# T5 attention and a max-of-three FFN on one core: head pairs on one array, bias as exponential factors in a band, replicated softmax sums, converting loads, and FFN chunks between score tiles

## The chip, the core and the metric

The kernel runs on one core of one Trainium2 chip. The core has TensorE (PE; its weight loads are listed as PEld), VectorE (DVE), ScalarE (ACT), GpSimd (POOL) and SyncE (SP); SP, ScalarE and POOL can issue DMAs. The metric is the device time of one execution in microseconds, the median of several runs.

## The reference

Attention with a T5 relative-position bias over 8 batches, 8 heads, 576 positions and a head size of 64, and behind it a feed-forward layer (FFN) whose hidden value is the largest of three products.

```
scores = q @ k.T / sqrt(64)                    # per batch and head, 576 x 576
n      = abs(i - j)
bucket = n                if n < 16
         16 + int(15 * log(n / 16) / log(8)), at most 31, otherwise
scores = scores + bias_table[bucket, head]
attn   = exp(scores - max) / (sum + 1e-9)
x      = (attn @ v), heads side by side        # 4608 tokens x 512
h      = max(x @ w1, x @ w2, x @ w3)           # 4608 x 768
out    = h @ w_out                             # 4608 x 512, float32
```

All inputs are float32. Both kernels compute in bfloat16 with float32 sums, and neither subtracts the maximum.

## The kernel before

Setup (L78 to L154). VectorE writes the bias of every distance, for 8 heads, into one row per head (L120); the row goes to DRAM (L127), and 40 transfers on SP and POOL bring it back as 40 bias tiles, one for each head and each of the five tiles of 128 keys (the last has 64), with keys in reverse order (L139). The four weights are loaded as float32 and converted by VectorE (L149, L154).

A head (`attention_head`, L158) runs in these steps.

- Loads: q on SP (L162, L165), k on ScalarE's queue (L166, L169), v on POOL (L170, L173), as float32; VectorE converts (L177 to L201).
- Transposes on TensorE: q against the identity (L186), k and v against a reversing matrix (L196, L207), each into the one PSUM buffer with the tag `tp`, copied out by VectorE or ScalarE (L191, L197, L208).
- For each of five key tiles: the scores, 128 keys by 576 queries, as matmuls of 512 and 64 columns that use 64 rows of the array (L215); VectorE adds the bias tile into float32 (L221); ScalarE takes the Exp into bfloat16 (L225); TensorE multiplies by v with a column of ones, 65 columns of the array, so that the last row of `ot` holds the sums (L229).
- Normalisation: VectorE copies the row of sums (L238), TensorE turns it into columns (L241), VectorE takes reciprocals and widens them to 64 columns (L247, L251), TensorE turns these back into rows (L257), ScalarE copies the outputs (L261), and VectorE multiplies (L264, L267) into `xT` and, for the last 64 tokens of the batch, into `xtail`.

The FFN of a batch is a list of 10 units: six first-stage units (L272: three products of four matmuls of 512 columns, L279, and the running maximum on VectorE, L287, L290, L293) and four second-stage units (L296: six matmuls, L301, a copy on ScalarE, L308, stores on SP, L310). `hook` (L346) runs one unit of the batch before behind every fourth score tile. Score tiles and FFN products share the two PSUM buffers of the tag `st`. The FFN of the last batch and that of the 512 tail tokens run at the end (L356, L358).

The order within each queue is made by the framework from the order of the program and its own estimate of when operands are ready; it also places the semaphores.

Of the kernel before, what the change touches and what calls it, by code (L numbers as in the profile page):

```python
# [39 lines left out]
def kernel(  # L41
# [17 lines left out]
    assert d_model == H * D and S == 576 and D == 64 and NB == 32  # L59
    NQT = 5  # L60
    WLEN = 2 * S - 1
    inv_sqrt_d = 1.0 / float(np.sqrt(D))
    KTILES = [(0, 128), (128, 128), (256, 128), (384, 128), (512, 64)]
    FCH = d_ff // 128
    DCH = d_model // 128
# [3 lines left out]
    biasp = ctx.enter_context(tc.tile_pool(name="biasp", bufs=1))  # L69
    headio = ctx.enter_context(tc.tile_pool(name="headio", bufs=2))  # L70
    headw = ctx.enter_context(tc.tile_pool(name="headw", bufs=2))
    xtp = ctx.enter_context(tc.tile_pool(name="xtp", bufs=2))
    ffnw = ctx.enter_context(tc.tile_pool(name="ffnw", bufs=2))
    psum = ctx.enter_context(tc.tile_pool(name="psum", bufs=1, space=bass.MemoryType.PSUM))
    psum2 = ctx.enter_context(tc.tile_pool(name="psum2", bufs=2, space=bass.MemoryType.PSUM))
    dram = ctx.enter_context(tc.tile_pool(name="dram", bufs=1, space=bass.MemoryType.DRAM))

    ident = const.tile([P, P], F32, name="ident")  # L78
    make_identity(nc, ident[:])
    ident_bf = const.tile([P, P], BF16, name="ident_bf")  # L80
    nc.vector.tensor_copy(ident_bf[:], ident[:])
    jrev = const.tile([P, P], BF16, name="jrev")
    jrev_f = const.tile([P, P], F32, name="jrev_f")
# [4 lines left out]
    )  # L88
    nc.vector.tensor_copy(jrev[:], jrev_f[:])
    jrev64 = const.tile([64, 64], BF16, name="jrev64")  # L90
    jrev64_f = const.tile([64, 64], F32, name="jrev64_f")
    nc.gpsimd.memset(jrev64_f[:], 0.0)
    nc.gpsimd.affine_select(
        out=jrev64_f[:], in_=jrev64_f[:], compare_op=ALU.not_equal, fill=1.0,
        base=-63, pattern=[[1, 64]], channel_multiplier=1,
    )
    nc.vector.tensor_copy(jrev64[:], jrev64_f[:])

    ones1 = const.tile([1, P], BF16, name="ones1")
    nc.vector.memset(ones1[:], 1.0)  # L100

    tableT = const.tile([H, NB], F32, name="tableT")
    tbl_src = bass.AP(
        tensor=bias_table.tensor, offset=bias_table.offset, ap=[[1, H], [H, NB]],
    )
    nc.sync.dma_start(out=tableT[:], in_=tbl_src)

    w_f = stage.tile([H, WLEN], F32, name="w_f", tag="w_f")
    nc.gpsimd.memset(w_f[:], 0.0)
    ranges = _bucket_ranges(S, NB, 128)  # L110
    for vv, rg in enumerate(ranges):
        if rg is None:
            continue
        lo, hi = rg
        segs = [(S - 1 + lo, S - 1 + hi)]
        lo2 = max(lo, 1)
        if hi > lo2:
            segs.append((S - 1 - hi + 1, S - 1 - lo2 + 1))
        for (m0, m1) in segs:
            nc.vector.tensor_scalar(  # L120
                out=w_f[:, m0:m1], in0=w_f[:, m0:m1], scalar1=tableT[:, vv : vv + 1],
                scalar2=8.0, op0=ALU.add, op1=ALU.mult,
            )
    w_sb = const.tile([H, WLEN], BF16, name="w_sb")
    nc.vector.tensor_copy(w_sb[:], w_f[:])
    w_dr = dram.tile([H, WLEN], BF16, name="w_dr")
    nc.sync.dma_start(out=w_dr[:], in_=w_sb[:])  # L127

    bias_tiles = [[None] * NQT for _ in range(H)]
    ei = 0  # L130
    for h in range(H):
        for t, (jt, kp) in enumerate(KTILES):
            bt = biasp.tile([P, S], BF16, name=f"bias_{h}_{t}", tag=f"bias_{h}_{t}")
            src = bass.AP(
                tensor=w_dr.tensor,
                offset=w_dr.offset + h * WLEN + (S - jt - kp),
                ap=[[1, kp], [1, S]],
            )
            (nc.sync if ei % 2 == 0 else nc.gpsimd).dma_start(out=bt[0:kp, :], in_=src)  # L139
            ei += 1  # L140
            bias_tiles[h][t] = bt

    w_bfs = []
    for wi, wk in enumerate((moe_w1, moe_w2, moe_w3)):
        st_w = stage.tile([P, DCH, d_ff], F32, name=f"wst{wi}", tag=f"wst{wi}")
        eng = nc.sync if wi % 2 == 0 else nc.scalar
        eng.dma_start(out=st_w[:], in_=wk.rearrange("(c p) f -> p c f", p=P))
        wb = const.tile([P, DCH, d_ff], BF16, name=f"w{wi}_bf")
        nc.vector.tensor_copy(wb[:], st_w[:])  # L149
        w_bfs.append(wb)  # L150
    wo_st = stage.tile([P, FCH, d_model], F32, name="wost", tag="wost")
    nc.gpsimd.dma_start(out=wo_st[:], in_=moe_w_out.rearrange("(c p) m -> p c m", p=P))
    wo_bf = const.tile([P, FCH, d_model], BF16, name="wo_bf")
    nc.vector.tensor_copy(wo_bf[:], wo_st[:])  # L154

    out_flat = out

    def attention_head(b, h, xT, xtail, hook):  # L158
        q_st = headio.tile([P, NQT, D], F32, tag="q_st")
# [45 lines left out]
        for t, (jt, kp) in enumerate(KTILES):  # L205
            jm = jrev if kp == 128 else jrev64
            nc.tensor.matmul(vr[0:kp, t, :], lhsT=jm[:, :], rhs=v_bf[0:kp, t, :])  # L207
# [182 lines left out]
```

## Time and profile before

| | |
|---|---|
| median of 3 runs | 1168.22 us (1166.13 to 1168.84) |
| profiled execution, first to last instruction | 1165.3 us |
| TensorE busy | 768.9 us, 66% |
| TensorE weight loads | 371.7 us, 32% |
| VectorE busy | 634.5 us, 54% |
| ScalarE busy | 320.6 us, 28% |
| POOL busy | 106.0 us, 9% |
| mean granted clock of TensorE | 0.740 |
| HBM read and written | 39.91 MB and 9.46 MB |

The page gives for the profiled execution its span alone, which is taken as its own time here. A row of the groups reads: line, engine, operation, output and inputs, shapes, count; then busy time in us and mean ns of one; then the engine's idle time before these instructions and what ended it. A row of the timeline reads: start, duration, engine, line, operation, count, and in brackets the idle time before it. Durations of consecutive matmuls overlap, so their pace is read from their starts. Shapes of matmuls begin with rows*columns of the array that they use.

### The profile page before, as it was taken

To read this page: it belongs to the slowest core of one execution; us is meant where nothing else is said; L and a number is where in the kernel's file an instruction comes from. 1 tells how busy PE (TensorE), PEld (TensorE's weight loads), DVE (VectorE), ACT (ScalarE), POOL (GpSimd) and SP (SyncE) were. 2 spreads that over 40 slices of the span, in tenths; PEclk is the share of its full clock that TensorE was granted. 3 is DMA by queue.
4 is the path that set the end of the run, shared out by engine and by line. 5 is a ranking of instruction groups with operands and counts; after the bars stand their busy time and mean duration, and the time that the engine had idled before them with its cause. 6 is when DMAs were issued, how large, how long until landed. Compare 5 with 4: busy or idle time off the path is not lost.

```text
span 1165.3 us, 11325 instructions
## 1 busy us (share of the span) xinstructions
PE 768.9 (66%) x3684; PEld 371.7 (32%) x3744; DVE 634.5 (54%) x1770; ACT 320.6 (28%) x485; POOL 106.0 (9%) x224
## 2 busy tenths in 40 slices
PE   0356666666667676666767666676766677676697
PEld 0123333333333333333333333333333333333333
DVE  4455555655555545564556545564555645565464
ACT  0233322232322232223322233222322233222311
POOL 2410000000000000000000000000000000000000
PEclk9999996765776667675667657766676756776599
DMA  7821111011101111101110111111111011100002
GB/s 247 195 65 32 30 31 31 16 40 49 35 21 31 35 49 30 29 18 50 49 26 21 31 47 41 26 26 36 52 31 26 21 49 49 26 21 1 18 27 64
DMA packets 94035, 50.12 MB, mean 43 GB/s; under 512 B 81488, under 2 KB 84816, under 8 KB 93976
## 3 DMA queue, kind: packets, MB, share of 16 engines
q1 hardware_dynamic: 48120, 24.71, 7.7%
q10 hardware_dynamic: 39440, 11.02, 4.1%
q0 software_dynamic: 6416, 13.67, 4.0%
q8 instruction: 29, 0.48, 0.2%
q14 instruction: 30, 0.25, 0.1%
HBM read 39.91 MB, written 9.46 MB: 42 GB/s over the span
## 4 chain that ended last, share of the span: by engine, by line
PE 51%; DVE 25%; ACT 9%; DMA 8%; issue 5%; ACTq 1%; SPq 0%; DVEq 0%; POOL 0%
PE ps L279 15%; PE ot L229 10%; DVE s_sb L221 7%; ACT e_bf L225 7%; DMA k_st<-in_k_dram 6%; PE tpq L186 4%; PE rb L257 4%; PE tpk L196 4%; PE st L215 4%; DVE xt L264 4%; DVE denrow L238 4%; DVE qT L191 2%; PE dcol L241 2%; ACT kT L197 2%; PE vr L207 2%
## 5 line engine op out<-in xcount | busy, mean ns | idle before, releaser
L225 ACT ACTIVATE e_bf<-s_sb 128x576 bf16<-128x576 f32 (+1 forms) x320 | 216.2, 682 | 367.3 <-DVE s_sb L221 220.0
L221 DVE TENSOR_TENSOR s_sb<-st,bias 128x576 f32<-128x576 f32 (+1 forms) x320 | 234.4, 753 | 94.1 <-PE st L215 81.1
L229 PE MATMUL ot<-e_bf,vb 128*65 128x512 bf16 (+3 forms) x640 | 173.3, 365 | 78.0 <-ACT e_bf L225 72.5
L215 PE MATMUL st<-qT,kT 64*128 64x512 bf16 (+3 forms) x640 | 171.9, 379 | 33.0 <-DVE s_sb L221 20.6
L279 PE MATMUL ps<-xt,w_bf 128*128 128x512 bf16 x540 | 176.7, 454 | 10.4 <-issue 5.9
L229 PEld LDWEIGHTS <-vb 128*65 128x65 bf16 (+1 forms) x640 | 80.4, 135 | 193.3 <-issue 184.5
L197 ACT ACTIVATE kT<-tpk 64x576 bf16<-64x576 f32 x64 | 41.2, 644 | 276.4 <-PE tpk L196 276.4
L186 PE MATMUL tpq<-ident_bf,q_bf 128*64 128x128 bf16 (+1 forms) x320 | 52.4, 302 | 94.1 <-DVE xtail L267 61.6
L170 POOL DMA_DIRECT2D v_st<-in_v_dram x64 | 50.6, 791 | 641.2 <-DVE v_bf L201 582.9
L279 PEld LDWEIGHTS <-w_bf 128*128 128x128 bf16 x648 | 63.8, 112 | 93.7 <-issue 54.3
L215 PEld LDWEIGHTS <-kT 64*128 64x128 bf16 (+1 forms) x640 | 53.7, 113 | 123.2 <-issue 115.7
L238 DVE CAST denrow<-ot 1x576 bf16<-1x576 f32 x64 | 48.1, 752 | 74.0 <-PE ot L229 73.8
L196 PE MATMUL tpk<-jrev,k_bf 128*64 128x128 bf16 (+1 forms) x320 | 49.3, 290 | 39.4 <-DVE qT L191 39.4
L287 DVE COPY cur<-ps 128x512 f32<-128x512 f32 x54 | 37.4, 692 | 69.3 <-PE ps L279 59.5
L257 PE MATMUL rb<-ident_bf,rrep 128*64 128x128 bf16 (+1 forms) x320 | 50.1, 278 | 35.4 <-DVE rrep L251 35.4
L186 PEld LDWEIGHTS <-q_bf 128*64 128x64 bf16 (+1 forms) x320 | 33.0, 151 | 113.0 <-DVE xtail L267 69.7
L207 PE MATMUL vr<-v_bf,jrev 128*128 128x64 bf16 (+1 forms) x320 | 35.9, 238 | 48.4 <-ACT kT L197 48.4
L264 DVE TENSOR_TENSOR xt<-o_sb,rb 64x512 bf16<-64x512 f32 x64 | 43.5, 680 | 35.0 <-PE rb L257 35.0
L261 ACT ACTIVATE o_sb<-ot 64x576 f32<-64x576 f32 x64 | 41.1, 643 | 76.8 <-DVE denrow L238 76.8
L208 DVE CAST vb<-vr 128x256 bf16<-128x256 f32 x64 | 27.3, 426 | 64.0 <-PE vr L207 64.0
L191 DVE COPY qT<-tpq 64x576 bf16<-64x576 bf16 x64 | 28.8, 450 | 56.5 <-PE tpq L186 56.5
L241 PE MATMUL dcol<-ones,denrow 1*128 1x1 bf16 (+1 forms) x320 | 24.1, 169 | 45.5 <-DVE denrow L238 45.5
(115 smaller groups left out, 580.8 us busy)
## 6 DMA issues: line engine op xcount, KB each, us to landing
k_st<-in_k_dram ACTq DMA_DIRECT2D x64, 128.0 KB, 2.2
v_st<-in_v_dram POOLq DMA_DIRECT2D x64, 128.0 KB, 2.7
q_st<-in_q_dram SPq DMA_DIRECT2D x64, 128.0 KB, 2.2
out_dram<-osb SPq DMA_DIRECT2D x32, 256.0 KB, 2.0
wst<-in_moe_w_dram SPq DMA_DIRECT2D x2, 1536.0 KB, 16.7
bias<-w_dr SPq DMA_DIRECT2D x16, 144.0 KB, 6.9
bias<-w_dr POOLq DMA_DIRECT2D x16, 144.0 KB, 8.0
wst<-in_moe_w_dram ACTq DMA_DIRECT2D x1, 1536.0 KB, 10.0
```

Source lines behind the costliest of these rows:

```text
L186: nc.tensor.transpose(tpq[:, 128 * t : 128 * t + rows], q_bf[0:rows, t, :], ident_bf[0:rows, 0:rows],)
L196: nc.tensor.matmul(tpk[:, jt : jt + kp], lhsT=k_bf[0:kp, t, :], rhs=jm[:, :])
L197: nc.scalar.activation(out=kT[:], in_=tpk[:], func=ACTF.Copy)
L207: nc.tensor.matmul(vr[0:kp, t, :], lhsT=jm[:, :], rhs=v_bf[0:kp, t, :])
L215: nc.tensor.matmul(st[0:kp, i0 : i0 + il], lhsT=kT[:, jt : jt + kp], rhs=qT[:, i0 : i0 + il],)
L221: nc.vector.tensor_tensor(out=s_sb[0:kp], in0=st[0:kp], in1=bias_tiles[h][t][0:kp], op=ALU.add,)
L225: nc.scalar.activation(out=e_bf[0:kp], in_=s_sb[0:kp], func=ACTF.Exp, scale=inv_sqrt_d)
L229: nc.tensor.matmul(ot[:, i0 : i0 + il], lhsT=vb[0:kp, t, :], rhs=e_bf[0:kp, i0 : i0 + il], start=(t == 0), stop=(t == NQT - 1),)
L238: nc.vector.tensor_copy(denrow[:], ot[D : D + 1, :])
L257: nc.tensor.matmul(rb[:, q0 : q0 + kq], lhsT=rrep[0:kq, t2, :], rhs=ident_bf[0:kq, 0:kq])
L264: nc.vector.tensor_tensor(out=xT[c][p0 : p0 + D, 0:512], in0=o_sb[:, 0:512], in1=rb[:, 0:512], op=ALU.mult,)
L279: nc.tensor.matmul(ps[:, 0:512], lhsT=w_bfs[ki][:, c, fs : fs + 128], rhs=xcols[c], start=(c == 0), stop=(c == DCH - 1),)
```

## The change

The attention and the order of the work are written anew; the FFN keeps its products.

- **Head pairs.** Two heads are handled together. q and k of a pair, 128 columns, are transposed in one go (10 transposes per pair, plain identity, no reversal; v isn't transposed). The scores of a tile of 128 keys are two matmuls of 288 queries: one head on rows 0 to 63 of the array, the other on rows 64 to 127, into two PSUM banks. Two halves of 288 queries times four key tiles make 8 such tiles per pair. The last 64 keys of both heads lie in a block-diagonal tile (`ktail`, `vtail`), whose scores for both halves are one more tile, with 128 rows.
- **Bias as factors.** exp(s + b) is computed as exp(s) times exp(b - b31), where b31 is the value of the last bucket; the constant falls out of the softmax. The factor is 1 outside a band of some 128 positions on either side of the diagonal, so VectorE multiplies only within the band (`band`, `bandt`), in place, in bfloat16. ScalarE takes the Exp straight from PSUM.
- **Replicated sums.** The sums are products with matrices of ones (64 columns, or block-diagonal for the last keys), so each stands in 64 rows. ScalarE takes Ln and then Exp of the negative, and VectorE multiplies the outputs. Sums and outputs of the two heads use columns 0 to 63 and 64 to 127 of the array.
- **Loads.** POOL issues all loads of q, k, v and the weights; they convert to bfloat16 on the way. A whole batch is loaded one batch ahead (17 DMAs; batch 0 pair by pair).
- **Order.** `attend` of a half is put off (`late`) and called between score tiles of the next half or pair. The FFN is cut into 9 chunks of 512 consecutive tokens, 22 units each (18 of four matmuls, 4 of six); `fill` adds three matmuls of credit behind each score tile and runs a unit when the credit reaches half its size. The first maximum's copy is ScalarE's and in bfloat16; the final copies alternate between VectorE and ScalarE. Chunks that become ready with the last batch (two) run at the end.

The core of the diff, new lines:

```
+    def load(b, h0, h1, tiles):
+        for src, dst in ((q, q_sb), (k, k_sb), (v, v_sb)):
+            for t in range(KT):
+                nc.gpsimd.dma_start(
+                    out=dst[:, t, h0:h1, :],
+                    in_=src[b, h0:h1, P * t : P * t + P, :].rearrange("h p d -> p h d"),
+                )
...
+    def fill(mms):
+        if not pending:
+            budget[0] = 0.0
+            return
+        budget[0] += mms
+        while pending and budget[0] >= pending[0][0] / 2:
+            n, u = pending.pop(0)
+            budget[0] -= n
+            u()
...
+    def scores(hp, qT, kT, c, t):
+        sc = ps_s.tile([P, 2, CH], F32, tag="sc", name="sc")
...
+            for par in range(2):
+                r = slice(64 * par, 64 * par + 64)
+                nc.tensor.matmul(
+                    sc[:, par, 0:QC], lhsT=kT[r, P * t : P * t + P], rhs=qT[r, c * QC : c * QC + QC]
+                )
...
+        nc.scalar.activation(out=e[:], in_=sc[:, :, 0:QC], func=ACTF.Exp, scale=inv_sqrt_d)
...
+                nc.vector.tensor_tensor(
+                    out=e[:, :, lo - c * QC : hi - c * QC], in0=e[:, :, lo - c * QC : hi - c * QC],
+                    in1=band[hp][:, :, lo - P * t + P : hi - P * t + P], op=ALU.mult,
+                )
...
+    def attend(b, hp, c, et, es):
+        nc.tensor.matmul(den[:, 0:QC], lhsT=onesd[:], rhs=et[:, c, :], start=True, stop=False,
+                         skip_group_check=True)
...
+        for dst in (den, o):
+            for t in range(KT):
+                for par in range(2):
+                    nc.tensor.matmul(
+                        dst[64 * par : 64 * par + 64, 0:QC],
+                        lhsT=ones[:] if dst is den else v_sb[:, t, 2 * hp + par, :],
+                        rhs=es[t][:, par, :], start=False, stop=(t == KT - 1),
+                        skip_group_check=True,
+                    )
+        nc.scalar.activation(out=ld[:], in_=den[:, 0:QC], func=ACTF.Ln)
+        nc.scalar.activation(out=rd[:], in_=ld[:], func=ACTF.Exp, scale=-1.0)
+        nc.vector.tensor_tensor(out=xT[hp][:, x0 : x0 + QC], in0=o[:, 0:QC], in1=rd[:], op=ALU.mult)
...
+            et = scores(hp, qT, kT, None, None)
+            fill(rate)
+            if late:
+                late.pop(0)()
+            for c in range(2):
+                es = []
+                for t in range(KT):
+                    es.append(scores(hp, qT, kT, c, t))
+                    fill(rate)
+                    if t == 1 and late:
+                        late.pop(0)()
+                    if c == 1 and t == 2 and not (b == B - 1 and hp == HP - 1):
+                        nxt = transposes(b + (hp + 1) // HP, (hp + 1) % HP)
+                late.append(lambda b=b, hp=hp, c=c, et=et, es=es: attend(b, hp, c, et, es))
+        if b < B - 1:
+            while late:
+                late.pop(0)()
+            for n in range(NCH):
+                if ready[n] == b:
+                    pending.extend(ffn_units(n))
```

`scores` has two score buffers of two PSUM banks each, `den` and `o` one bank each, and FFN products, transposes and the band share the last two. The table set of ScalarE that holds both Exp and Ln is loaded by name at the start.

More of the change, by code (lines that the diff above doesn't have):

```diff
@@ L124 @@
[L124 to L141, printed above, removed]
@@ new lines @@
+    for hp in range(HP):
+        make_band(hp)
+    ready = {n: (n * CH + CH - 1) // S for n in range(NCH)}
+    nxt = transposes(0, 0)
+    late = []
+    for b in range(B):
+        if b + 1 < B:
+            batch[b + 1] = load_tiles()
+            load(b + 1, 0, H, batch[b + 1])
+        for hp in range(HP):
+            qT, kT = nxt
+            rate = 27.0 / 9
+            et = scores(hp, qT, kT, None, None)
[4 more added lines that the diff above has]
+                es = []
+                for t in range(KT):
+                    es.append(scores(hp, qT, kT, c, t))
[11 more added lines that the diff above has]
+                    pending.extend(ffn_units(n))
@@ L356 @@
+    while late:
+        late.pop(0)()
+    for n in range(NCH):
+        if ready[n] == B - 1:
+            pending.extend(ffn_units(n))
     while pending:
-        pending.pop(0)()
-    for u in ffn_tail_units(xtail):
-        u()
+        pending.pop(0)[1]()
 _INS = ['q', 'k', 'v', 'bias_table', 'moe_w1', 'moe_w2', 'moe_w3', 'moe_w_out']
```

427 lines of the change are left out of this document (194 added, 233 removed).

## The prediction

> **What bounds the kernel now.** I read the page first (busy times and the chain that ended last), then the chain in order of time, then TensorE's timeline across one head.
>
> ```profile
> span 1165.3 us, 11325 instructions
> ...
> PE 768.9 (66%) x3684; PEld 371.7 (32%) x3744; DVE 634.5 (54%) x1770; ACT 320.6 (28%) x485; POOL 106.0 (9%) x224
> ...
> PE 51%; DVE 25%; ACT 9%; DMA 8%; issue 5%; ACTq 1%; SPq 0%; DVEq 0%; POOL 0%
> ```
>
> No engine is busy for more than 66% of the span, and the chain passes from engine to engine: this is latency, not throughput. From the chain in order of time, the same FFN burst in two successive batches:
>
> ```profile
> 217.31 2.77 PE ps L279 x6
> ...
> 354.05 2.77 PE ps L279 x6
> ```
>
> One batch with FFN work takes 136.7 us. From TensorE's timeline, in batch 0, where no FFN runs:
>
> ```profile
> 99.60 0.64 PE L229 MATMUL ot<-e_bf,vb 64*65 64x512 bf16 x2 [0.58 <-ACT e_bf L225]
> ...
> 103.78 0.82 PE L186 MATMUL tpq<-ident_bf,q_bf 128*64 128x128 bf16 x5 [0.97 <-DVE xtail L267]
> ...
> 107.14 1.14 PE L215 MATMUL st<-qT,kT 64*128 64x512 bf16 x4
> ...
> 113.58 0.64 PE L229 MATMUL ot<-e_bf,vb 64*65 64x512 bf16 x2 [0.59 <-ACT e_bf L225]
> ```
>
> The last attention product of a head starts at 99.60, the next head's first scores at 107.14: for 7.5 of the 14.0 us per head the sums, the reciprocal, the broadcast, the normalisation and the next head's transposes follow each other, one small step at a time, each waiting for another engine.
>
> **The change, part by part.** The serial part between heads goes: sums come out already replicated over 64 rows, the reciprocal becomes Ln and Exp on ScalarE, and the normalisation of one pair of heads runs between the score tiles of the next. So engines should be limited by their work, which I sum per batch (4 head pairs, 36 score tiles). Prices, from the groups by form:
>
> ```profile
> L221 DVE TENSOR_TENSOR s_sb<-st,bias 128x576 f32<-128x576 f32 x256 | 187.3, 754 | 87.6 <-PE st L215 77.9 <-ACT e_bf L225 5.1 <-DMA bias<-w_dr 3.2
> ...
> L170 POOL DMA_DIRECT2D v_st<-in_v_dram x64 | 50.6, 791 | 641.2 <-DVE v_bf L201 582.9 <-DVE q_bf L177 34.3 <-issue 23.9
> ...
> L264 DVE TENSOR_TENSOR xt<-o_sb,rb 64x512 bf16<-64x512 f32 x64 | 43.5, 680 | 35.0 <-PE rb L257 35.0
> ...
> L197 ACT ACTIVATE kT<-tpk 64x576 bf16<-64x576 f32 x64 | 41.2, 644 | 276.4 <-PE tpk L196 276.4
> ...
> L290 DVE TENSOR_TENSOR nxt<-cur,ps 128x512 f32<-128x512 f32 x54 | 37.1, 688 | 30.6 <-PE ps L279 30.2
> ...
> L173 POOL DMA_DIRECT2D v_st<-in_v_dram x64 | 33.9, 530 | 0.0
> ...
> L191 DVE COPY qT<-tpq 64x576 bf16<-64x576 bf16 x64 | 28.8, 450 | 56.5 <-PE tpq L186 56.5
> ...
> L197 ACT ACT_TABLE_LOAD x1 | 1.3, 1283 | 34.9 <-DMA q_st<-in_q_dram 34.9
> ```
>
> And, from the timeline, a ScalarE copy of 512 elements:
>
> ```profile
> 1155.56 0.60 ACT L308 ACTIVATE osb<-ops__9207 128x512 f32<-128x512 f32 x1 [16.88 <-PE ops__9207 L301]
> ```
>
> ScalarE: an Exp now reads PSUM, as the L197 copy of 576 elements does (0.644 us): 36 x 0.644 = 23.2. A Ln and an Exp of 288 elements for each of 8 normalisations, at 0.43 (0.644 less 288 elements at the 0.74 ns by which the two copies differ): 6.9. FFN copies, 8 at 0.60: 4.8. Sum 34.9 us. The Ln waits for the sums; behind it in ScalarE's queue stand the next Exps, and for those TensorE's next scores but one.
>
> VectorE: the bias additions go. Per pair: two transposed copies at 0.45 and 0.48 (L191, and 640 elements at the same slope), two normalising products of 288 at 0.45 (L264 less 224 elements at 1.04 ns), eight band products of 2,880 elements in all. No band product is in the trace; its bounds are the f32 rate of L221 (1.04 ns per element plus 0.15 each: 4.2) and half of that per element, as L191 shows for bf16 (2.7). That is 4.5 to 6.0 per pair, 18 to 24 per batch; with 14 FFN operations at 0.69, 28 to 34 us.
>
> TensorE is then the largest. The end of the trace gives it at full speed with nothing in its way:
>
> ```profile
> 1137.72 16.45 PE L279 MATMUL ps<-xtail,w_bf 128*128 128x512 bf16 x71
> 1154.01 1.46 PE L301 MATMUL ops__9207<-wo_bf,hT 128*128 128x512 bf16 x6
> ...
> 1157.90 1.46 PE L301 MATMUL ops__9240<-wo_bf,hT 128*128 128x512 bf16 x6
> ```
>
> From 1154.01 to 1157.90 three groups of six matmuls of 512 columns start, 1.30 us each: 0.216 each, 0.42 ns per column, so 0.1215 for 288 columns. One FFN chunk runs from 1137.72 to 1159.2: 21.5 us. A pair of heads needs 10 transposes (five take 0.82 with the last one's latency; I take 0.1 each: 1.0), 6 products over the whole array (0.73) and 48 that use half of it: 16 for scores (64 rows), 32 for sums and outputs (64 columns), issued in twos on opposite halves. No two matmuls overlap in this trace, so a two costs between 0.1215 and 0.243. What switching between shapes costs, and how fast loads can follow, stands here (timeline, TensorE at full clock):
>
> ```profile
> 1110.39 0.41 PE L229 MATMUL ot<-e_bf,vb 128*65 128x512 bf16 x2 [0.37 <-ACT e_bf L225]
> ...
> 1110.72 0.43 PE L215 MATMUL st<-qT,kT 64*64 64x512 bf16 x2
> ...
> 1111.11 0.41 PE L229 MATMUL ot<-e_bf,vb 128*65 128x512 bf16 x2
> ...
> 1111.35 0.81 PE L301 MATMUL ops__8888<-wo_bf,hT 128*128 128x512 bf16 x2
> ...
> 1114.55 0.28 PEld L241 LDWEIGHTS <-denrow 1*128 1x128 bf16 x5 [0.62 <-DVE denrow L238]
> ```
>
> 576 columns take 0.24 when the next matmul also uses all rows (1111.11 to 1111.35), but 0.33 when a 64-row one follows (1110.39 to 1110.72): about 0.1 us per switch. The change switches twice at each of 8 half-array score tiles of a pair and about four times more: 20 x 0.1 = 2.0 (bound: 0). The five loads of L241 with their matmuls follow at 0.046, so two need 0.09, less than 0.1215: the instruction stream does not force a two apart, and its halves share neither rows and columns nor, for scores, the bank. I therefore take 0.15, near the low end: 24 x 0.15 = 3.6. The Trainium skill ("TensorE: Matmul & The Clock Gate", Part 3 on packing small matmuls) has matmuls on disjoint tiles start about 4 ns apart; by that a two would cost some 0.126, an estimate, and the total below would be 16 us lower. No run here shows it yet.
>
> So a pair costs TensorE 1.0 + 0.73 + 3.6 + 2.0 = 7.33, four cost 29.3, the chunk beside them 21.5, and at the end of a batch the last normalisations are flushed with nothing else queued (one Exp, one band product and the products: about 1.5). A batch takes 52.3 us, with ScalarE (34.9) and VectorE (34) inside it. In TensorE's queue the attention products of one pair stand ahead of the next scores; while they run, two score buffers keep ScalarE going for 1.3 us, which is enough only while TensorE is the slower of the two.
>
> This needs the full clock. Four stretches of a head in the middle (columns: PE, PEld, DVE, ACT, POOL busy, then the granted clock):
>
> ```profile
> 648.00:651.00 3.00, 2.78 (x10) 1.27 (x10) 0.85 (x2) 1.21 (x2) 1.32 (x2) 0.50 0.01 1
> 651.00:654.00 3.00, 2.54 (x13) 0.99 (x12) 2.17 (x4) 0.00 (x0) 0.00 (x0) 0.96 0.17 53
> 654.00:658.00 4.00, 1.32 (x12) 0.85 (x11) 2.13 (x9) 1.33 (x2) 0.12 (x1) 1.00 0.00 0
> 658.00:662.00 4.00, 1.75 (x12) 1.26 (x13) 1.95 (x7) 0.64 (x1) 0.00 (x0) 0.51 0.02 5
> ```
>
> The clock rises behind stretches with TensorE 93% busy and falls to half behind one with 33%. At half clock the changed kernel asks more of TensorE than a batch holds, so it is saturated, and the clock should rise and stay.
>
> Loads: q, k and v move from three queues to POOL's alone, converted on the way, one batch ahead: 17 issues per batch, 13,824 runs of 256 bytes. The queue that loaded k (columns: packets, MB, share of 16 engines):
>
> ```profile
> q10 hardware_dynamic: 39440, 11.02, 4.1%
> ```
>
> POOL needs 0.53 for 64 runs (L173) and 0.79 for 512 (L170), so 16.5 us per batch by that line. The runs of the k queue cost 4.1% of 16 x 1165.3 us over 39,440 packets: 19.4 ns each, 16.8 us per batch over 16 engines. No converting load is in the trace; they stay hidden up to 52.3 x 16 / 13,824 = 60 ns a run, three times the row; I take the row. ScalarE's queue issues no loads any more, and SP's only the stores. The Trainium skill ("DMA: Bandwidth & Descriptors", Specifications) says that pieces under 512 bytes are written by read-modify-write; doubling the row for that, an estimate, gives 34 us, still hidden. VectorE's conversions and the stores of tails in pieces (8 of the 40) go at no further cost.
>
> Start and batch 0, from the timeline, and the first 20 us as one stretch (last column: GB/s):
>
> ```profile
> 19.68 8.54 DVE L120 TENSOR_SCALAR w_f<-w_f,tableT 8x1 f32<-8x1 f32 x63
> ...
> 33.01 25.04 SPq L139 DMA_DIRECT2D bias<-w_dr  x20
> ```
>
> ```profile
> 0.00:20.00 20.00, 0.00 (x0) 0.00 (x0) 4.30 (x9) 0.00 (x0) 6.11 (x18) 1.00 0.91 304
> ```
>
> The 40 bias tiles (20 of them 25 us of issue on SP) become one transfer of 0.8 MB. The band is ready after 61 small copies (8.3 us at L120's pace), two transfers through DRAM (an estimate: 0.8 MB of the 5.3 MB that took those 25 us, and as much again for their fixed part, 7) and the products behind a first load of the table, at about 23 us. The loads of pair 0 take POOL 10.4 us (17 issues of 0.53 to 0.64), and those of each further pair as long, so pair 3 has its data at about 46 and batch 0 ends at 57. Then 6.3 MB of weights (21 us at the 304 GB/s of the first stretch) lie ahead of batch 1's loads, so that its first pair starts at about 70.
>
> End: the last batch leaves two chunks, 43 us; from the last matmul (1159.3) to the end of the span took 6 us, and still does.
>
> Sum: 70 + 7 x 52.3 + 43 + 6 = 485 us. The span of the profiled execution, 1165.3, stands 0.25% below the median of 1168.22, which I leave out.
>
> **The rivals.**
> Twos run one after the other (chance 0.22): nothing in the trace overlaps. Then 54 x 0.1215 = 6.56 + 3.0, four times, + 21.5 + 1.5 = 61.3 per batch: 548. In this case the array is not shared, which is what the change says it does.
> No switch cost and full overlap (0.08): 4 x (30 x 0.1215 + 1.0) + 21.5 = 40.1 per batch, 5 us above ScalarE: 400.
> The clock stays at half (0.07): the monitor may see less in half-array products. Chunk and products double: 2 x 21.5 + 4 x (2 x 4.33 + 1.0) = 81.6 per batch, 690. Against it: the burst at 648 mixed 64-row and full products and raised the clock.
> Converting loads take 80 ns a run (0.05): 69 us per batch: 602.
> Ln and Exp reload the table each time (0.04): 16 x 1.28 = 20.5 more on ScalarE, 55 per batch: about 505. The change loads one set at the start; before, Copy and Exp needed one load.
> Slower than before (0.02): the same loads, priced so that they bound all batches. That needs (1165 - 49) / 8 = 139.5 us per batch, 161 ns a run, eight times the row; at 180 ns it would be 156 us per batch: 1,295 us.
>
> **How the numbers follow.** The forecast, 485, has 0.52. The range 415 to 580 holds it with its unknown terms, the one-after-the-other case, the reloads and a part of the fast case: about 0.8. A difference of 0.2% is about what a measurement of this kernel can tell from none. Faster by more than that 0.97, within it 0.01, slower 0.02.
>
> **What would show it.** Right: batches of some 52 us; TensorE above 90% busy there at a clock near 1.00; twos of 64-row matmuls starting close together; ScalarE near 35 and VectorE near 30 us per batch; no wait for q, k or v after batch 1 begins; a tail of 43 us. Wrong: twos 0.12 apart and 61 us per batch; a clock near 0.5; TensorE waiting on load tiles; ScalarE with many table loads; or ScalarE as the engine that TensorE waits for, which would mean that the order of the queues, not the sum of the work, sets the pace.

## The result and the profile after

The changed kernel takes 447.26 us (median of 4 runs, 446.27 to 448.24), the kernel before, run beside it, 1167.18. The ratio is 0.3832, 95% interval 0.3823 to 0.3841. The profiled execution took 446.27 us, of which 444.5 are its span.

From the profile's page: span and instructions, busy time of each engine, the granted clock in 40 slices, the queue of the converting loads (packets, MB, share of 16 engines), and the chain that ended last by engine.

```profile
span 444.5 us, 7552 instructions
...
PE 401.0 (90%) x2881; PEld 186.6 (42%) x2928; DVE 229.7 (52%) x587; ACT 266.3 (60%) x494; POOL 145.7 (33%) x199
...
PEclk9999966999999999999999999999999999999999
...
q0 software_dynamic: 115952, 17.31, 54.6%
...
PE 81%; POOL 10%; DMA 5%; issue 2%; DVE 1%; ACT 0%; POOLq 0%
```

The chain no longer passes from engine to engine: 81% of it is TensorE, at full clock except in two slices, between 55 and 78 us. The chain in order of time shows the start, one point of the FFN in three successive batches, the last such point and the tail:

```profile
13.63 2.83 POOL q_sb L107 x4
...
24.96 2.89 POOL q_sb L107 x4
...
48.13 10.28 DMA w_bf<-in_moe_w_dram
58.69 12.56 DMA k_sb<-in_k_dram
72.23 1.07 PE ps L219 x2
...
109.38 1.29 PE ps L243 x6
...
155.38 1.29 PE ps L243 x6
...
201.38 1.29 PE ps L243 x6
...
385.88 1.29 PE ps L243 x6
...
439.59 0.82 PE ps L243 x3
```

A batch takes 46.0 to 46.1 us ((385.88 - 109.38) / 6), where the kernel before took 136.7; this time per batch is called the period below. A stretch of 10 us in the gap at the start and one of 50 us in the middle (columns: PE, PEld, DVE, ACT, POOL busy, granted clock, DMA share, which exceeds 1 where the times of packets overlap, and GB/s):

```profile
60.00:70.00 10.00, 0.86 (x3) 0.31 (x3) 0.00 (x0) 0.00 (x0) 3.87 (x5) 0.50 1.78 181
110.00:160.00 50.00, 49.17 (x380) 23.46 (x384) 28.02 (x67) 34.44 (x65) 17.32 (x22) 1.00 0.71 68
```

In the gap nothing works but transfers and POOL's issues, and the granted clock is 0.50. In the middle TensorE is busy for 98% of the time. Scaled to 46.1 us, ScalarE works 31.7 us per batch, VectorE 25.8, POOL 16.0. TensorE's timeline across one half of a head pair shows how it works:

```profile
199.19 0.66 PE L338 MATMUL o<-e,v_sb 128*64 128x288 bf16 x8
199.78 0.30 PE L307 MATMUL sc<-qT,kT 64*128 64x288 bf16 x2
200.00 0.40 PE L279 MATMUL tq<-ident,q_sb 128*128 128x128 bf16 x4
...
201.21 1.46 PE L243 MATMUL ps<-wo_bf,hT 128*128 128x512 bf16 x6
202.51 0.41 PE L300 MATMUL sc<-qT,kT 128*128 128x288 bf16 x2
202.75 0.29 PE L333 MATMUL o<-et,vtail 128*128 128x288 bf16 x1
202.97 0.68 PE L338 MATMUL den<-e,ones 128*64 128x288 bf16 x8
203.48 0.66 PE L338 MATMUL o<-e,v_sb 128*64 128x288 bf16 x8
204.07 0.30 PE L307 MATMUL sc<-qT,kT 64*128 64x288 bf16 x2
```

Two things are to be read here. Eight products over half the columns start at 202.97 and the next group at 203.48: 0.51 us, so a two (two products on opposite halves of the array) costs 0.1275, little more than one product (0.12: the two over the whole array at 202.51 take 0.24). And where the shape changes, time is added: from 203.48 to 204.07 the same eight take 0.59, a two of scores ahead of transposes takes 0.22 (199.78 to 200.00) in place of 0.1275, and one whole-array product ahead of the sums 0.22 (202.75 to 202.97) in place of 0.12. A change of shape costs some 0.095 us in either direction.

In the groups by form, the small terms and the single load of ScalarE's table:

```profile
L311 ACT ACTIVATE e<-sc 128x576 bf16<-128x576 f32 x256 | 159.0, 646 | 31.0 <-PE sc L307 28.0
...
L349 DVE TENSOR_TENSOR xT<-o,rd 128x288 bf16<-128x288 f32 x64 | 29.2, 456 | 38.8 <-ACT rd L347 38.8
L321 DVE TENSOR_TENSOR e<-e,band 128x576 bf16<-128x576 bf16 x64 | 29.1, 455 | 6.1 <-ACT e L311 3.5
...
L86 ACT ACT_TABLE_LOAD x1 | 1.3, 1283 | 0.7 <-PEq L405 0.7
```

The waits of VectorE for `rd` and of ScalarE for `sc` are idle time of engines that have room; they cost nothing.

### The profile page after: what moved, and what is told of

It is laid out like the page before. It is cut to its first block, busy times and chain, and to the rows that moved or that the text cites. A ratio compares the mean times of both kernels' runs of the same rounds, so it can differ in the third digit from the quotient of the medians.

```text
span 444.5 us, 7552 instructions
## 1 busy us (share of the span) xinstructions
PE 401.0 (90%) x2881; PEld 186.6 (42%) x2928; DVE 229.7 (52%) x587; ACT 266.3 (60%) x494; POOL 145.7 (33%) x199
## 3 DMA queue, kind: packets, MB, share of 16 engines
q0 software_dynamic: 115952, 17.31, 54.6%
## 4 chain that ended last, share of the span: by engine, by line
PE 81%; POOL 10%; DMA 5%; issue 2%; DVE 1%; ACT 0%; POOLq 0%
PE ps L219 34%; PE ps L243 11%; PE sc L307 10%; PE den L338 9%; PE o L338 6%; DMA k_sb<-in_k_dram 3%; POOL q_sb L107 3%; POOL k_sb L107 3%; PE den L331 3%; POOL v_sb L107 2%; DMA w_bf<-in_moe_w_dram 2%; PE tk L287 2%; PE sc L300 2%; PE o L333 2%; PE tq L279 2%
## 5 line engine op out<-in xcount | busy, mean ns | idle before, releaser
L311 ACT ACTIVATE e<-sc 128x576 bf16<-128x576 f32 x256 | 159.0, 646 | 31.0 <-PE sc L307 28.0
L219 PE MATMUL ps<-xT,w_bf 128*128 128x512 bf16 x617 | 163.3, 383 | 4.5 <-issue 2.3
L321 DVE TENSOR_TENSOR e<-e,band 128x576 bf16<-128x576 bf16 (+5 forms) x224 | 79.5, 356 | 55.4 <-ACT e L311 48.5
L107 POOL DMA_DIRECT2D q_sb<-in_q_dram x44 | 37.1, 918 | 139.2 <-PE tq L280 108.5
L307 PE MATMUL sc<-qT,kT 64*128 64x288 bf16 x512 | 69.9, 294 | 1.0 <-ACT et L311 0.7
L338 PE MATMUL den<-e,ones 128*64 128x288 bf16 x512 | 57.6, 298 | 0.3 <-DVE e L321 0.3
L228 DVE TENSOR_TENSOR m<-ps,m 128x512 bf16<-128x512 f32 x54 | 37.2, 688 | 31.9 <-PE ps L219 25.2
L243 PE MATMUL ps<-wo_bf,hT 128*128 128x512 bf16 x200 | 49.7, 380 | 1.6 <-issue 1.1
L338 PE MATMUL o<-e,v_sb 128*64 128x288 bf16 x512 | 48.9, 289 | 0.0
L231 DVE TENSOR_TENSOR hT<-ps,m 128x512 bf16<-128x512 f32 x54 | 37.1, 687 | 4.6 <-PE ps L219 3.3
L311 ACT ACTIVATE et<-sc 128x576 bf16<-128x576 f32 x32 | 20.7, 647 | 21.5 <-PE sc L300 21.5
L243 PEld LDWEIGHTS <-hT 128*128 128x128 bf16 x216 | 19.4, 98 | 22.9 <-issue 2.2
```

Of the source, the lines that this page charges most:

```text
L107: nc.gpsimd.dma_start(out=dst[:, t, h0:h1, :], in_=src[b, h0:h1, P * t : P * t + P, :].rearrange("h p d -> p h d"),)
L219: nc.tensor.matmul(ps[:], lhsT=w_bf[ki][:, c, cf * P : cf * P + P], rhs=xT[c][:, t0 : t0 + CH], start=(c == 0), stop=(c == DCH - 1),)
L228: nc.vector.tensor_tensor(out=m1[:], in0=ps[:], in1=st["m"][:], op=ALU.max)
L231: nc.vector.tensor_tensor(out=hT[:, cf, :], in0=ps[:], in1=st["m"][:], op=ALU.max)
L243: nc.tensor.matmul(ps[:], lhsT=hT[:, cf, tcn * P : tcn * P + P], rhs=wo_bf[:, cf, :], start=(cf == 0), stop=(cf == FCH - 1),)
L307: nc.tensor.matmul(sc[:, par, 0:QC], lhsT=kT[r, P * t : P * t + P], rhs=qT[r, c * QC : c * QC + QC])
```

## The experiments

All were run beside the kernel before; ratios are to that. My theory: TensorE's own work sets the batch (products, overlapped in twos, plus 0.095 per change of shape), and everything else is hidden behind it; only the start is set by loads. The rivals differ by run.

**Do twos overlap because the code issues opposite halves in turn?** The loops over key tiles and heads are exchanged, so that four products on one half stand ahead of four on the other.

```
-            for t in range(KT):
-                for par in range(2):
+            for par in range(2):
+                for t in range(KT):
```

> The sums and outputs of one half are issued head by head (four products on columns 0 to 63, then four on columns 64 to 127) instead of alternating; work and operands are the same. Theory that opposite halves overlap: of 16 half-array products per normalisation 13 now take 0.1215 us each instead of 8 twos at 0.128, so 1.58 us instead of 1.03, 0.55 us more for each of the 56 normalisations in batches 1 to 7: about 31 us longer, 478 us, batch period 50.5 us. Rival that a half-array product is simply cheap, whatever its neighbour: no change, 447 us within 1%.

Measured: 456.5 us, ratio 0.3913 [0.3907, 0.3920]. Both missed. The timeline of TensorE:

```profile
203.81 0.69 PE L338 MATMUL den<-e,ones 128*64 128x288 bf16 x8
204.33 0.68 PE L338 MATMUL o<-e,v_sb 128*64 128x288 bf16 x8
```

Eight still take 0.52 us, though the compiled program has them in groups of four: products for the free half start ahead of products that were issued before them. Over five batches the mean step from one half-column product to the next is 70.8 ns in place of 58.9, with 115 such steps per batch: 1.4 us, about the 1.25 per batch by which this version is slower. Of the 128 such products of a batch 52 start within 31 ns of the one before, against 62 in the changed kernel: where other work breaks up a group, ten more products find no partner and take their 0.12 us alone. The Trainium skill ("TensorE: Matmul & The Clock Gate", Part 3, on what overlaps and what doesn't) says that matmuls keep strictly to program order; this trace differs, for products on opposite halves.

**Is the overlap what makes the twos cheap?** Both heads write the same half of the columns, so that the second head's sums and outputs are added to the first's (that part of the result changes).

```
-                        dst[64 * par : 64 * par + 64, 0:QC],
+                        dst[0:64, 0:QC],
```

> Sums and outputs of both heads go to columns 0 to 63, so the two heads are added together there and rows 64 to 127 of the sums hold the last keys' part alone; count, size and order of the instructions are the same. Theory that opposite halves overlap even when not alternated (so the order alone could not undo it): on one half, 16 products take 1.94 us instead of 1.03 per normalisation, 0.9 us more for 56 of them in batches 1 to 7, 51 us longer, about 498 us. Rival that half-array products are short by themselves: 447 us within 1%.

Measured: 496.22 us, ratio 0.4257 [0.4249, 0.4265]. As the theory says. The same place of the timeline:

```profile
203.31 1.17 PE L338 MATMUL den<-e,ones 128*64 128x288 bf16 x8
204.32 1.14 PE L338 MATMUL o<-e,v_sb 128*64 128x288 bf16 x8
```

Now eight take 1.01 us, one after the other. This is the rival of the prediction in which the array is not shared, made real for the sums and outputs: sharing their columns is worth 49 us.

**Do the scores gain from sharing rows?** The contraction takes all 128 rows, which adds the two heads' scores (that part of the result changes); two whole-array products in place of a two.

```
-                r = slice(64 * par, 64 * par + 64)
+                r = slice(0, 128)
```

> Each score product reads all 128 rows instead of 64, so the two heads' scores are added together in the result; order and count of instructions are the same. Theory that a two of 64-row scores overlaps but pays a change of shape on the way in or out (0.1215 + 0.11): two products on all rows take 0.243 and no change of shape, so the time stays within 1% of 447 us. Rival A, overlap without a price for the change of shape: 0.12 us more for 224 score tiles of batches 1 to 7, 27 us longer, 474 us. Rival B, scores of 64 rows never overlapped: no change either, but then 64-row products that follow each other directly would be 0.12 us apart in the trace.

Measured: 445.08 us, ratio 0.3819 [0.3811, 0.3826]; the same or 2 us less.

```profile
109.80 1.34 PE ps L243 x6
...
201.67 1.34 PE ps L243 x6
```

As the theory says: the period is 45.9 ((201.67 - 109.80) / 2). Counted from TensorE's records, a batch has 34 changes of shape in place of 74. At 0.097 those 40 are worth 3.9 us; 64 whole products at 0.1215 in place of 32 twos at 0.1275 cost 3.7. Rival B, that score products never overlap, is out as well. Where two score twos follow each other in the changed kernel, all four products take 0.42 us, where the first two alone take 0.30:

```profile
205.70 0.42 PE L307 MATMUL sc<-qT,kT 64*128 64x288 bf16 x4
```

The score twos share the array and gain nothing by it, since most of them stand alone between two changes of shape (21 of the 32 per batch have no other score two beside them).

**Can they stand together?** Two score tiles are issued one after the other, with the FFN fill of both behind them.

```
-                for t in range(KT):
+                for t in range(0, KT, 2):
                     es.append(scores(hp, qT, kT, c, t))
-                    fill(rate)
+                    es.append(scores(hp, qT, kT, c, t + 1))
+                    fill(2 * rate)
```

> Two score tiles are issued together, then twice the FFN credit. Theory that each change of shape costs about 0.11 us: four of eight changes per pair go, 0.44 us for each of 28 pairs in batches 1 to 7, up to 12 us shorter, 435 to 441 us (the framework's order already puts some tiles together). Rival that two score buffers leave ScalarE short when TensorE does six FFN products in a row: same or slower, 447 to 460 us.

Measured: 448.28 us, ratio 0.3846 [0.3838, 0.3854]: no gain. The edit did a part of what it was for: of the 32 score twos of a batch 23 now stand beside another, where 11 did. But a batch still has 70 changes of shape in place of 74. The transposes of q's last rows, which use 64 rows of the array too, no longer stand beside a score two, and the sums and outputs are broken up once more. What it would bring if the other changes did not come back was therefore not tried.

**Do the loads cost anything once batches run?** From batch 2 on, the tiles of the batch before last are used again (the results of those batches change).

```
-        if b + 1 < B:
+        if b == 0:
             batch[b + 1] = load_tiles()
             load(b + 1, 0, H, batch[b + 1])
+        elif b + 1 < B:
+            batch[b + 1] = batch[b - 1]
```

> Only batches 0 and 1 are loaded; later batches compute with their data again, so the output is that of two batches repeated. Theory that loads are hidden from batch 1 on: 447 us within 1%, batch period 46.1 us. Rival that the loads on POOL and the 16 DMA engines slow the other engines or the batches: shorter by 2 us or more per batch, below 435 us.

Measured: 447.08 us, ratio 0.3836 [0.3824, 0.3847]. The stretch of 50 us:

```profile
110.00:160.00 50.00, 49.17 (x380) 23.48 (x386) 28.00 (x67) 34.50 (x66) 0.00 (x0) 1.00 0.07 27
```

POOL does nothing and the DMA share falls from 0.71 to 0.07, while TensorE's 49.17 stays to the digit. From batch 2 on the loads are fully hidden.

**What is the interleaving worth?** No FFN units between score tiles; the whole chunk follows a batch's attention.

```
-                    fill(rate)
...
+            while pending:
+                pending.pop(0)[1]()
```

> The FFN chunk of a batch runs as a block behind the next batch's attention instead of in pieces between its score tiles. Theory that interleaving hides ScalarE's work behind TensorE's: alone, the attention of a batch is set by ScalarE (about 28 us of work, 30 with waits) instead of TensorE (25), and the chunk (21 us) comes on top: 51 us per batch instead of 46, 35 us longer for seven batches, about 480 us. Rival that TensorE sets the pace in either order: 447 us within 1%.

Measured: 475.4 us, ratio 0.4079 [0.4073, 0.4085]. Two stretches, one of FFN and one of attention:

```profile
110.00:120.00 10.00, 10.00 (x45) 4.29 (x44) 4.61 (x7) 2.98 (x6) 4.26 (x6) 1.00 0.93 59
...
140.00:150.00 10.00, 9.81 (x95) 4.92 (x95) 6.12 (x18) 9.50 (x20) 7.17 (x9) 1.00 1.85 118
```

ScalarE is 30% busy beside the FFN and 95% busy in the attention, and it has 10% of the chain that ended last, where it had 0%. The same work, apart, takes 28 us more; the theory had 35. ScalarE is not shown to be the only reason: the view of waits lists a single wait of TensorE for it in the 250 us from 110 on (0.6 us), and a batch has 90 changes of shape in place of 74, some 1.6 us of the 4.0 that each batch is longer.

**The start.** TensorE's wait in the changed kernel, from the timeline:

```profile
66.97 0.29 PE L279 MATMUL tq<-ident,q_sb 128*128 128x128 bf16 x1 [11.96 <-DMA q_sb<-in_q_dram]
```

Batch 1's loads stand behind the weights on POOL, whose own issues of k wait too, three times some 3 us, until a weight has landed. Here batch 0's pairs 1 to 3 come in one set, and the weights go as float32 over SP's queue as soon as `hank` is there; VectorE converts them.

```
-    for hp in range(1, HP):
-        load(0, 2 * hp, 2 * hp + 2, batch[0])
+    load(0, 2, H, batch[0])
...
+        nc.vector.tensor_copy(wst[0:1, 0, 0:1], hank[0:1, 0, 0:1])
+        nc.sync.dma_start(out=wst[:], in_=wk.rearrange("(c p) f -> p c f", p=P))
+        nc.vector.tensor_copy(wb[:], wst[:])
```

> Batch 0 is loaded as pair 0 and then pairs 1 to 3 together, and the weights come as float32 over SP once the band data has landed, and are converted by VectorE; batches 1 to 7 as before. Theory that the first 72 us are set by POOL's issue (46 us for batch 0) and by the weights standing ahead of batch 1's loads: batch 0 ends at about 46 and batch 1 starts at 48 to 55 us, 17 to 24 us shorter, 423 to 431 us. Rival that the DMA engines, with converting loads at 33 ns a run, are what fills the start: batch 1 starts at about 68 us, 441 to 447 us.

Measured: 440.97 us, ratio 0.3781 [0.3774, 0.3789]: the edge of the rival's range, with the first FFN products of batch 1 at 65.3 us where they were at 71.4. The stretch from 20 to 30 us, and TensorE's waits in it:

```profile
20.00:30.00 10.00, 0.56 (x4) 0.10 (x1) 2.27 (x3) 0.00 (x0) 0.89 (x2) 1.00 1.16 356
```

```profile
24.63 0.29 PE L281 MATMUL tq<-ident,q_sb 128*128 128x128 bf16 x1 [4.37 <-DMA q_sb<-in_q_dram]
31.06 0.29 PE L281 MATMUL tq<-ident,q_sb 128*128 128x128 bf16 x1 [6.14 <-DMA q_sb<-in_q_dram]
35.65 0.29 PE L281 MATMUL tq<-ident,q_sb 128*128 128x128 bf16 x1 [4.30 <-DMA q_sb<-in_q_dram]
```

The weights now take the DMA engines (356 GB/s) while batch 0's own loads wait for them: the gap has moved from batch 1 to batch 0. Next, the weights are held back until batch 0's v has landed, by a one-element copy on POOL, and converted between batch 0's pairs.

```
+        nc.gpsimd.tensor_copy(wst[0:1, 0, 0:1], batch[0][2][0:1, KT - 1, H - 1, 0:1])
+        nc.sync.dma_start(out=wst[:], in_=wk.rearrange("(c p) f -> p c f", p=P))
...
+            if b == 0 and hp >= 2:
+                for wi in (2 * hp - 4, 2 * hp - 3):
+                    nc.vector.tensor_copy(w_bf[wi][:], wsts[wi][:])
```

> The start again: batch 0's pairs 1 to 3 come in one set of loads, and the weights (float32, over SP's queue) are held back by a one-element copy on POOL until batch 0's v has landed; VectorE converts them between the pairs of batch 0. Theory (the start is set by the order in which loads take POOL and the 16 DMA engines): pairs 1 to 3 have their data at about 25 us instead of 46, batch 0 is then limited by ScalarE (7.5 us a pair, from about 15 to 50), the weights land at about 50, the first FFN group of batch 1 runs 16 to 22 us earlier than in the changed kernel, the period stays 46, and the time is 425 to 431. Rival (something else holds the start, POOL's issues of batch 1 or the conversions): 437 to 445, as with the weights that came too early.

Measured: 442.41 us, ratio 0.3794 [0.3787, 0.3801]: in the range of the rival, by which something else holds the start. From the timeline, and one stretch of 10 us:

```profile
38.62 0.23 PE L280 MATMUL tq<-ident,q_sb 128*128 128x128 bf16 x1 [4.00 <-DMA q_sb<-in_q_dram]
46.96 0.29 PE L280 MATMUL tq<-ident,q_sb 128*128 128x128 bf16 x1 [8.12 <-DMA q_sb<-in_q_dram]
...
52.00 0.29 PE L280 MATMUL tq<-ident,q_sb 128*128 128x128 bf16 x1 [4.37 <-DMA q_sb<-in_q_dram]
...
62.79 0.66 PE L301 MATMUL sc<-qT,kT 128*128 128x288 bf16 x2
```

```profile
50.00:60.00 10.00, 7.59 (x42) 2.94 (x44) 1.68 (x5) 4.26 (x8) 7.71 (x10) 0.50 2.13 138
```

By 34 us batch 0 is through half of its scores, and all its pairs are transposed. Then TensorE stands at the transposes of batch 1, whose q waits behind the weights. In TensorE's queue they stand ahead of most scores of batch 0's last two pairs, which follow only then (the last pair's first at 62.79), at a granted clock of 0.50. So work for TensorE was there, and the order of its queue kept it waiting. VectorE's conversions hold little: VectorE waits 1.9 us for the first weight, and is then idle for 15.9 us, until 55.45. In these three orders a gap of 12 to 16 us behind the weights changes its place, and the order is worth 5 to 6 us. What later transposes of batch 1 would bring was not tried.

**Scores over all rows with the right result.** Each head's keys stand in a tile of their own whose other 64 rows are zero, on top of the first start. One difference comes with it: the weights' float32 tiles share two buffers in turn, where the first start had four.

```
+            nc.vector.tensor_copy(kT[r, par, :], tk[r, 0 : KT * P])
...
-                    sc[:, par, 0:QC], lhsT=kT[r, P * t : P * t + P], rhs=qT[r, c * QC : c * QC + QC]
+                    sc[:, par, 0:QC], lhsT=kT[:, par, P * t : P * t + P], rhs=qT[:, c * QC : c * QC + QC]
```

> The start of the run before, and in addition each head's keys stand in 128 rows with the other head's rows zero, so that scores are full-array products without a change of shape; VectorE writes the transposed keys in three copies instead of one (0.6 us more per pair). Theory from the runs before (a two of 64-row scores takes 0.324 us with its two changes of shape, two products on all rows 0.246): another 2 us less than the run with the new start alone. Rival that the longer way to the first scores of a pair costs as much: the same within 1 us, or longer.

Measured: 440.6 us, ratio 0.3779 [0.3772, 0.3786], the same as without it, but as the sum of two changes. In the chain the period is 46.8 at first and 46.4 later, longer than the 46.0 to 46.2 of the first start alone and not shorter, and the same FFN point of batch 1 comes 5 us earlier. The stretch from 30 to 40 us, without the zero rows and with them:

```profile
30.00:40.00 10.00, 3.46 (x18) 1.51 (x18) 1.14 (x3) 1.19 (x2) 4.71 (x7) 1.00 1.76 231
...
30.00:40.00 10.00, 9.24 (x71) 5.31 (x69) 7.18 (x15) 7.37 (x13) 10.00 (x10) 0.73 1.39 217
```

With two buffers the third weight is issued at 33 us and the last at 40, where all four were issued by 17, and TensorE is busy in that stretch for 9.24 us and not 3.46. The spread weights are the likely reason for the shorter start; they were not tried alone. So the start can gain more than the three orders above show; here the longer period takes the gain back.

**Less work for TensorE.** VectorE adds the four score tiles of a half (each addition rounded to bf16), and one two sums the result in place of four.

```
+                    if t:
+                        esum = esp.tile([P, 2, QC], BF16, tag=f"es{t}", name="esum")
+                        nc.vector.tensor_tensor(
+                            out=esum[:], in0=es[0][:] if t == 1 else prev[:], in1=es[t][:], op=ALU.add
+                        )
+                        prev = esum
```

> VectorE adds the four score tiles of a half (bf16), and TensorE sums the result with one two in place of four; everything else as in the changed kernel. Theory (TensorE's own work sets the batch): 3 twos of 0.1275 go for each of 8 halves, 24 x 0.1275 = 3.06 us per batch, the period falls from 46.0 to 43.0 and the time by 7 x 3.06 = 21 us, to 424 to 428; VectorE rises from 26 to about 37 us per batch and stays inside. Rival (the queues' order sets the pace: the sums now wait for the last addition, and a longer VectorE queue holds the band products and transposed copies): period 45 or more, 440 us or slower.

Measured: 436.04 us, ratio 0.3742 [0.3737, 0.3748], between the two. The chain, and the stretch of 50 us:

```profile
149.75 1.40 PE ps L244 x6
...
194.66 1.40 PE ps L244 x6
...
328.10 1.40 PE ps L244 x6
...
372.36 1.40 PE ps L244 x6
```

```profile
110.00:160.00 50.00, 49.35 (x342) 20.99 (x339) 38.14 (x96) 35.21 (x69) 18.39 (x23) 1.00 0.79 73
```

The period falls to 44.9, in the last batches to 44.3, by half of the 3.06 us that were taken from TensorE. Is VectorE's chain of additions the reason? In the next run the tiles are added in twos only, two additions that don't depend on each other, and two twos sum them.

```
+                    if t % 2:
+                        esum.append(esp.tile([P, 2, QC], BF16, tag=f"es{t}", name="esum"))
+                        nc.vector.tensor_tensor(
+                            out=esum[-1][:], in0=es[t - 1][:], in1=es[t][:], op=ALU.add
+                        )
```

> Score tiles are added in twos only (2 additions per half in place of 3, none depending on another), and TensorE sums with two twos in place of four: it saves 16 x 0.1275 = 2.04 us per batch, 14 us in all. With three additions only half of the 3.06 us per batch that TensorE was spared showed in the period. Theory (the other half went into waits behind VectorE's chain of additions): with the chain gone nearly the whole 14 us show, 433 to 435 us. Rival (half of it is lost wherever it comes from, in TensorE's changes of shape and the order of its queue): 439 to 441 us.

Measured: 438.59 us, ratio 0.3765 [0.3759, 0.3772]: in neither range, 0.4 us below the rival's; 8.7 of 14 us show, where 11.2 of 21 did. So the chain of additions is not what loses most of the rest. Counted from the records of the run with all four added, the steps between half-column products fall by 3.03 us per batch as priced; some 0.85 comes back ahead of whole-array products (the view of waits names `xT` and `hT`, results of the fuller VectorE, for 0.35 of it) and some 0.65 at changes of shape, of which there are 2 more. Why the order shifts so was not settled.

Last, the first start and the sums together. For room the weights' float32 tiles share two buffers in turn, and the sums have two buffers of each kind in place of three. The second start and the sums do not fit into SBUF together, so that pair was not measured.

> The first start (batch 0's pairs 1 to 3 in one set, weights as float32 over SP's queue) together with the sums added first on VectorE. Alone they took 447.3 to 441.0 and to 436.0. Theory (start and period are independent terms of the sum): the gains add, 428 to 432 us. Rival (with shorter batches and a fuller VectorE the start's gain is lost again): 434 us or more.

Measured: 433.67 us, ratio 0.3724 [0.3709, 0.3739], with runs from 432.1 to 435.9: the fastest version here, 3.0% below the changed kernel, and 4 us short of the sum of the gains. It lies between the two ranges, and the buffers are a difference besides, so neither case is shown. The profiled execution, 434.87 us, shows where its gain went:

```profile
148.68 1.40 PE ps L246 x6
...
193.59 1.40 PE ps L246 x6
```

The period is the 44.9 of the sums alone, and the same FFN point comes 1.1 us earlier than there (149.75), where the first start alone had gained 5. So in this execution it is the start that loses its gain, and not the period.

## Why the prediction came out as it did

Its mechanism held: latency went, TensorE's work became the bound, and the time fell within the range, 38 us below the forecast. The experiments bear that out: work added to TensorE came on top nearly in full (49 us where 51 were expected, with the columns not shared), and loads taken away changed nothing. But of work taken from TensorE only half to 0.6 came off the time, so its work is not all that sets the pace. The parts of the change (bias as factors, replicated sums, head pairs, converting loads) were not timed one at a time against the kernel before. Where those 38 us were, by its own sum against the profiled span of 444.5:

- Start, 70: measured 72.2 (the first FFN products of batch 1 in the chain), by the steps it named: POOL's issues, 11.3 us per pair (24.96 - 13.63) against 10.4, then the weights, then batch 1's loads. Right, but in part by luck: four times 10.4 is 41.6 and not the 46 at which the last pair was to have its data, the prediction does not say what the other 4 us are, and the slower issues took as much (4 x 11.3 = 45.3). That the clock falls to 0.50 in the gap was not in it.
- Batch, 52.3: measured 46.1. This step was mis-sized, by 7 x 6.2 = 43 us, more than the whole error. Its terms: the twos at 0.1275 and not 0.15 (96 x 0.0225 = 2.2 us). The transposes follow at a median of 56 ns and not at 100 (40 x 0.044 = 1.8): the prediction took them from five with the last one's latency in them. The flush at a batch's end, 1.5, is not there: between its products stand FFN products and the first scores of the next batch, and TensorE has no wait of that length. The changes of shape are 74 and not 80, at 0.095 to 0.1: right within 1 us. The chunk beside attention is 96 products at 0.216, 20.8 and not the 21.5 that held the gaps of a tail (0.7). Together 2.2 + 1.8 + 1.5 + 0.8 + 0.7 = 7.0, of which 0.8 is not there; TensorE is idle for as much (0.83 of the 50 us above).
- Tail, 43, and end, 6: seven periods from 72.2 end at 394.9; from there it is 45.5 us to the end of the last product (439.59 + 0.82) and 4.1 to the end of the span. Together 49.6 against 49.

On the twos the Trainium skill's rule of some 4 ns between disjoint tiles ("TensorE: Matmul & The Clock Gate", Part 3) would have given 0.126: the trace agrees, 0.1275. The prediction kept to 0.15 since no row of the trace before showed an overlap; the experiment with the same columns shows that the overlap is there and what it is worth. The price of a change of shape, read from two rows of the trace before, was the best-founded of the new costs and held; the Trainium skill ("TensorEngine Tiling (Array Packing)", Key Properties) says that a change of tiling mode drains the engine; the trace fits that, at 0.095 us a change, though no row shows the drain itself.

The other engines: ScalarE 31.7 against 34.9 (Exp 646 ns against 644, but successive ones overlap a little), VectorE 25.8 against 28 to 34, since the band products run at the low bound (455 ns for 576 elements). POOL 16.0 against 16.5. The converting loads take 33.5 ns a packet, the larger ones of the weights included (54.6% of 16 x 444.5 us over 115,952), not the 19.4 of the row taken, still below the 60 at which they would show; taking them away changed nothing. By packets that is 28.9 us per batch: the Trainium skill's rule of the read-modify-write of pieces under 512 bytes ("DMA: Bandwidth & Descriptors", Specifications), by which the prediction had estimated 34, was nearer than the row; no run shows that this is the reason.

The rivals: the one-after-the-other case is out (0.51 for eight), and so is full overlap without a price for changes, whose 400 us had nothing for the 7 us per batch that the changes of shape cost. The clock stayed at 1.00 in the batches, and the table was loaded once.

## What to carry to other kernels

Where TensorE has become the bound, count its changes of shape as well as its products: a half-array two that stands alone between whole-array products costs more than the two whole products that it replaces would (0.1275 + 2 x 0.095 = 0.32 against 0.24 us), while a run of them is nearly twice as fast. Interleave an engine-heavy stage between the steps of another so that both engines work at once. When a gap stands at the start, see what each queue holds behind the instruction that waits: bytes that must move anyway only move the gap, while work that is ready behind a waiting transpose could fill it.

## What the runs showed of the hardware

Products on the free half of the columns overtake products that were issued ahead of them for the busy half (eight in 0.52 us, issued in groups of four). A change of shape costs 0.095 to 0.1 us in both directions, whether rows or columns change. Converting loads of 256-byte runs take some 32 ns a packet here (the run with two batches' loads has 84,576 packets fewer, at 31.7 ns each by the queue's share), and loads queued behind a large converting transfer on the same queue wait for it (TensorE waited 12 us for the first q of batch 1).
